# The gradients dK and dV of an attention block: dK on eight array tiles, two shared PSUM banks, and other places for three projections

## The chip, the core and the metric

The kernel runs on one core of a Trainium2 chip. A core has a tensor engine (PE, with its weight loads shown as PEld), a vector engine (DVE), a scalar engine (ACT), GpSimd (POOL), a queue engine that issues most transfers (SP), and 16 DMA engines. Each engine takes its instructions in order and waits on semaphores for the others. PE multiplies a stationary operand of up to 128 rows by 128 columns, loaded beforehand, by a moving operand that is streamed column by column, and writes into PSUM, eight banks of 128 partitions x 512 fp32 values. Its array can be used as tiles: a tile of 32x128 takes 32 rows of the contraction, a tile of 128x32 gives 32 output partitions, and sixteen tiles of 32x32 each have 32 rows and 32 output partitions of their own. Matmuls on different tiles can run at the same time.

The metric is the device time of one execution in microseconds (us).

## The reference

Two blocks read x (1 x 2048 x 448 each), and their outputs are concatenated. The kernel computes the outputs and all gradients for a given grad_out. Block A is linear attention with 16 heads; it is done in the first 205 us and is not touched. Block B is softmax attention with 16 query heads of 28 channels that share one key and one value head:

```
q = (x @ wq) as 16 heads;  k = x @ wk;  v = x @ wv          # one k, one v
p = softmax(q k^T * 28 ** -0.5);  o = p v;  out = o @ wo
# backward, with do = grad_out @ wo^T by head:
dV = sum over heads p^T do          dP = do v^T
dS = p * (dP - rowsum(do * o))      dQ = dS k        dK = sum over heads dS^T q
dx, dwq, dwk, dwv, dwo from dQ, dK, dV, o and x
```

All matmul operands are bf16, sums are fp32.

## The kernel before, in words

**Blocks and units.** The 2048 queries and 16 heads of block B are cut into 64 blocks, each of 256 queries and two heads. A block is worked off in eight units of 256 keys, so the main loop (L926) has 512 units of scores, numbered u, and 28 more in which the lagging steps run out. Loop and order of every engine are written out by hand (`tc.manual_schedule`, L917): the engines execute what the loop body issues, in that order. It runs from about 207 to 1017 us.

**One unit.** `rows_SD` (L683) issues eight matmuls on 32x128 tiles: the scores S of unit u for two heads, and dP of unit u-16. S of the first head goes to one of three banks SB (index 2u mod 3), of the second to the next of them; dP goes to the two banks DB. ACT takes the exponential of the first head's scores (L946), copies the second head's dP to SBUF as cp (L960), and takes the exponential of the second head (L992): three operations of 128x512 a unit. DVE multiplies the first head's dP by the stored exponentials (L958) and POOL the second head's cp (L961); both halves make dsT, the transposed dS. DVE transposes dsT in 32x32 blocks into dsx (L1039) for dK. Every fourth unit SP issues a DMA transpose of the exponentials, eT to eN (L994), for dV. In even units the second head's dP comes last in `rows_SD`.

**What follows in odd and even units.** In odd units come the four dK steps of `dk_m` (L860), for dsx of an older block (unit u-27), each four matmuls on four 32x32 tiles, 512 keys wide, all into the bank dk_acc. After the 32x32 transposes row group a of dsx holds, as rows, 32 queries, and as columns the keys 32a to 32a+31 of each 128; so the tile of row group a yields 32 channels of dK for 512 of the 2048 keys, in the output partitions from 32a. In even units come `o_dq` (L889: O and dQ on 128x32 tiles) and, at three of every four, one or two dV steps of `dv_mm` (L896), four matmuls on 128x32 tiles, 512 keys wide, into a bank dv_acc. Also in even units stand the PE transposes of O (`onat_T`, L809, u mod 8 = 2) and of do (`don_T`, L840, u mod 8 = 6) and the parts of the out-projection (L733). These use the score bank that is free at that time, `spare` = SB[(2u+2) mod 3] (L932), which is also the bank of the next unit's first scores.

**The do-projection.** do = grad_out @ wo^T is computed in 16 row tiles (`do_proj`, L903, and its copy to SBUF on DVE, `do_copy`, L913). Tiles 0 to 12 are done whole, four 128x512 matmuls, in the odd units 1 to 25; tiles 13 to 15 by quarters of 128 columns, 16 matmuls on 128x32 tiles each, in the units 32, 40, ... 120. The table is `do_slots` (L915). Before unit 16 the banks DB serve, then dk_acc until unit 27, then `spare` (L942).

**Transposes for dK's other operand.** For later blocks POOL copies queries into a staging tile qst (L851) at units 30, 31, 38, 39, 46, 47, 54, 55 of each 64; SP transposes it into qX behind the eN transposes in its queue.

**The end.** From unit 519 on, no scores are left, and dK uses a second bank, dk_two (SB[2]): the steps of odd m go to other output partitions of that bank, so that eight tiles work at a time. Matmuls for wo's gradient (`gwo`, L783, evicted at L793 and stored at L796) fill PE, and loads and transposes for the last stage are issued by SP. dv_acc is copied out at unit 533 (L1024, ACT), dk_two at unit 536 (L1030, ACT). After the loop dk_acc and the copy of dk_two are added in four DVE operations (L1059) into dkvT. Then rows of it are put into dQ's tile by 14 transfers (L1100, half on SP, half on POOL), and PE does `dwq` (L1063), the transposes of dK and dV, `dx` and the gradients of wk and wv.

Which tile of the array a dK matmul takes, and where it writes, is in this call:

```
mmt((dk_two if other else dk_acc)[k:k + 32, :],
    qX[qc][32 * a:32 * a + 32, B, s, pair * 64 + 32 * h:pair * 64 + 32 * h + 32],
    rhs, (32 * a, k), ...)        # (first row, first column) of the 32x32 tile
```

Of the kernel before, what the change touches and what calls it, by code (L numbers as in the profile page):

```python
# [8 lines left out]
ACT = mybir.ActivationFunctionType  # L9
ALU = mybir.AluOpType  # L10
AX = mybir.AxisListType
BF16 = mybir.dt.bfloat16
F32 = mybir.dt.float32
# [4 lines left out]
P = 128  # L18
# [7 lines left out]
def kernel(  # L26
# [21 lines left out]
    nc = tc.nc  # L48
# [3 lines left out]
    scale = float(DH) ** -0.5  # L52
# [586 lines left out]
    psA = psc.enter_context(tc.tile_pool(name="psA", bufs=4, space=bass.MemoryType.PSUM))  # L639
# [7 lines left out]
    NB = 64  # L647
# [3 lines left out]
    with ExitStack() as cs_:  # L651
        pe_ = cs_.enter_context(tc.tile_pool(name="ceT", bufs=1, side="right"))
        pn_ = cs_.enter_context(tc.tile_pool(name="ceN", bufs=1, side="right"))
        pd_ = cs_.enter_context(tc.tile_pool(name="cdsT", bufs=5, side="right"))
# [6 lines left out]
        SB = [psA.tile([P, 512], F32, name="aacc") for i in range(3)]  # L661
        DB = [psA.tile([P, 512], F32, name="agen") for i in range(2)]
        oq, dk_acc = (psA.tile([P, 512], F32, name="agen") for _ in range(2))

        dsT, dsx, qX, don, doT, rl, prod = ({} for _ in range(7))
# [6 lines left out]
        def eN(b, c):  # L672
            return ENs[(2 * b + c // 2) % 6][:, 16 * (c % 2):16 * (c % 2) + 16, :]

        def mmt(out, lhsT, rhs, pos, start, stop):
            nc.tensor.matmul(out, lhsT=lhsT, rhs=rhs, start=start, stop=stop, tile_position=pos,  # L676
                             skip_group_check=True)

        def blk(b):
            qc, pair = divmod(b, 8)  # L680
            return qc, pair, pair // 2, pair % 2
# [72 lines left out]
        post = {"gb": [], "xb": []}  # L754
# [100 lines left out]
            nc.sync.dma_start_transpose(qX[qc].rearrange("p b s c -> p (b s) c")[:, :, g * P:(g + 1) * P],  # L855
                                        st.rearrange("p n a j -> p (n a j)"))

        dk_two = SB[2]

        def dk_m(b, m, other=0):  # L860
            qc, pair, g, hp = blk(b)
            h, B, s = m // 8, (m // 2) % 4, m % 2
            for a in range(4):
                rhs = dsx[b][32 * a:32 * a + 32, :, h, :, :].rearrange(
                    "p u t (b i s) -> p u t b i s", b=4, s=2)[:, :, :, B, :, s]
                k = 32 * ((a + 2) % 4) if other else 32 * a
                mmt((dk_two if other else dk_acc)[k:k + 32, :],
                    qX[qc][32 * a:32 * a + 32, B, s, pair * 64 + 32 * h:pair * 64 + 32 * h + 32],
                    rhs, (32 * a, k), other == 2 or b == 0 and m == 0, other == 0 and b == NB - 1 and m == 15)

        def o_mm(v):
            b, tp = divmod(v, 8)
# [16 lines left out]
        def o_dq(vs, ys):  # L889
            for v, y in zip(vs, ys):  # L890
                todo = [f(i) for f, i in ((o_mm, v), (dq_mm, y)) if 0 <= i < NU]
                for _ in range(2):
                    for g_ in todo:
                        next(g_)

        def dv_mm(dv_acc, b, h, qb):  # L896
            for c in range(4):
                rhs = eN(b, c).rearrange("p (u h t q) k -> p u h t q k", u=2, h=2,
                                                       t=2)[:, :, h, :, qb, :]
                mmt(dv_acc[32 * c:32 * c + 32, :], don[b][:, qb, h, :], rhs, (0, 32 * c),  # L900
                    b == 0 and h + qb == 0, b == NB - 1 and h + qb == 2)

        def do_proj(i, c0, c1, ps):  # L903
            for c in range(4):
# [7 lines left out]
        def do_copy(i, c0, c1, ps):  # L912
            nc.vector.tensor_copy(out=do_nat[:, i, c0:c1], in_=ps[:, 0:c1 - c0])  # L913

        do_slots = {2 * i + 1: (i, 0, 512) for i in range(13)}  # L915
        do_slots.update({32 + 8 * n: (13 + n // 4, n % 4 * P, n % 4 * P + P) for n in range(12)})
        with tc.manual_schedule():  # L917
            nc.sync.dma_start(wo, wo_d[:, 0:D].rearrange("(g p) c -> p g c", p=P))
            qX[0] = pqa_.tile([P, 4, 2, 512], BF16, name="qX")
# [6 lines left out]
            for u in range(NU + 28):  # L926
# [5 lines left out]
                spare = SB[(2 * u + 2) % 3] if hasS else DB[u // 4 % 2] if u > 530 else SB[2]  # L932
# [6 lines left out]
                    out_proj(*op, spare)  # L939
                dpj = do_slots.pop(u, None)  # L940
                if dpj is not None:
                    dps_ = DB[u // 2 % 2] if u < 16 else dk_acc if u < 27 else spare  # L942
                    do_proj(*dpj, dps_)

                if hasS:
# [1 line left out]
                if u == 1:  # L947
                    q_shift(pn3, shifts[3], [pd_.tile([P, 2, 512], BF16, name="dsT").rearrange("p a b -> p (a b)").bitcast(F32)
                                             for _ in range(1)])
                    dv_acc = psA.tile([P, 512], F32, name="aacc")  # L950
                if u == 11:
                    for n in (2, 3):
                        put_shift(nc.sync, shifts[n], slice(n * 512, n * 512 + 512))
# [21 lines left out]
                if (b := due(u, 27)) is not None:  # L975
                    qc, pair, g, hp = blk(b)
                    nc.vector.tensor_scalar(out=qT_B[g][64 * hp:64 * hp + 64, qc * 256:(qc + 1) * 256],
                                            in0=oq[64:128, 0:256], scalar1=scale, scalar2=None, op0=ALU.mult)
# [20 lines left out]
                if u % 2:  # L999
                    b, i = divmod(u - 27, 8)  # L1000
                    if 0 <= b < NB:
                        for m in range(2 * i, 2 * i + 4):
                            dk_m(b, m, (1 + (u == 519 and m == 2 * i + 1)) * (m % 2) if 519 <= u < 537 else 0)
                else:
                    o_dq((u - 2, u - 1), (u - 20, u - 19))
                    b, n = divmod(u - 20, 8)
                    for k in {0: (0, 1), 2: (2,), 6: (3,)}.get(n, ()) if 0 <= b < NB else ():
                        dv_mm(dv_acc, b, k // 2, k % 2)
                y = u - 18

                if 512 <= u < 528 and u % 2 == 0:
# [6 lines left out]
                for v, half, gs in ((523, 0, (0, 1)), (525, 0, (2, 3)), (527, 1, (0, 1)), (529, 1, (2,)), (531, 1, (3,))):  # L1018
                    for g_ in gs if u == v else ():
                        nc.sync.dma_start_transpose(dqn[half][:, :, g_ * P:(g_ + 1) * P],  # L1020
                                                    qT_B[g_][:, half * 1024:half * 1024 + 1024])
                if u == 533:
                    for c in range(4):
                        nc.scalar.activation(out=post["dkvT"][32:64, c * 512:(c + 1) * 512], in_=dv_acc[32 * c:32 * c + 32, :],  # L1024
                                             func=ACT.Copy)
                if u == 536:
                    dk_sum = pd_.tile([P, 2, 512], BF16, name="dsT").rearrange("p a b -> p (a b)").bitcast(F32)
                    for c in range(2):
                        r = 64 * (1 - c)
                        nc.scalar.activation(out=dk_sum[64 * c:64 * c + 64, :], in_=dk_two[r:r + 64, :], func=ACT.Copy,  # L1030
                                             scale=scale)
                if u >= 519:
                    gwo(GW[u - 519], GW[u - 518])

                if 0 <= y < NU:
                    b, tp = divmod(y, 8)
                    if tp == 0:
                        dsx[b] = px_.tile([P, 8, 2, 2, 256], BF16, name="dsx")
                    nc.vector.transpose(  # L1039
                        out=dsx[b][:, tp, :, :, :].rearrange("p h t c -> p (h t c)").bitcast(F32),  # L1040
                        in_=dsT[y][:, :, :].rearrange("p h c -> p (h c)").bitcast(F32))

        dkvT, wqT, xb = post["dkvT"], post["wqT"], post["xb"]
# [10 lines left out]
            return pd_.tile([P, 2, 512], BF16, name="dsT")[:, 0, :]  # L1054

        for c in range(4):
            t = dkvT[0:32, :].rearrange("p (t a i) -> p t a i", a=4, i=32)[:, :, c, :]
            src = dk_acc[32 * c:32 * c + 32, :].rearrange("p (t i) -> p t i", i=32)
            nc.vector.scalar_tensor_tensor(out=t, in0=src, scalar=scale,  # L1059
                                           in1=dk_sum[32 * c:32 * c + 32, :].rearrange("p (t i) -> p t i", i=32),  # L1060
                                           op0=ALU.mult, op1=ALU.add)

        def dwq(c):  # L1063
            r = DC_ROWS[c]
# [44 lines left out]
        for c in range(4):  # L1109
            r = DC_ROWS[c]  # L1110
            ps = gen(0)
            for st in range(NS):
# [3 lines left out]
                                 func=ACT.Copy)  # L1116
# [35 lines left out]
```

## Time and profile before

| | |
|---|---|
| median of 3 runs | 1054.08 us (1053.51 to 1054.29) |
| profiled execution | 1052.68 us |
| its span | 1050.9 us |
| granted TensorE clock | 1.00 |
| PE busy | 1008.4 us, 96% |
| DVE busy | 895.9 us, 85% |
| ACT busy | 871.5 us, 83% |
| POOL busy | 798.2 us, 76% |
| dK matmuls of 32x512 into dk_acc | 4024 in the trace, 376 ns each, 264.0 us busy |
| dV matmuls of 128x512 | 1024, 379 ns each, 96.7 us busy |

A row of a group gives its line, engine, operation, the tiles written and read, the shape, the number of instructions, then busy time, mean duration of one, and the idle time of the engine ahead of them with what ended it. Matmuls overlap one another, on tiles above all, so a matmul's duration is not the time that it adds: the distance between starts is. The same holds for ACT and DVE operations, whose durations reach into the next operation. A timeline row gives the start within the span, the duration, and the group, where neighbours of one kind are put together with their number.

### The profile page before, as it was taken

The page shows a single profiled execution, that of the slowest core. Times are in us where ns is not written, and L with a number is a line of the kernel's source. Part 1 is how long each engine was busy: PE and PEld are TensorE (multiplying, and loading weights), DVE is VectorE, ACT ScalarE, POOL GpSimd, SP SyncE. Part 2 cuts the span into 40 slices and gives each one's busy share as a digit, 9 for nine tenths or more (in the row PEclk, how much of TensorE's full clock was granted, in tenths as well). Part 3 has the DMA queues.
Part 4 walks back from the last instruction along what each step waited for, and adds up shares of the span by engine and source line. Part 5 has one row for each costly group of instructions (what it writes and reads, how often), then busy time and mean ns, then how long its engine had stood idle before and what let it go on. Part 6 is the DMA issues. An engine that isn't in the chain of part 4 may idle for free.

```text
span 1050.9 us, 40033 instructions
## 1 busy us (share of the span) xinstructions
PE 1008.4 (96%) x16236; PEld 486.6 (46%) x16245; DVE 895.9 (85%) x1781; ACT 871.5 (83%) x1743; POOL 798.2 (76%) x1044
## 2 busy tenths in 40 slices
PE   9999999998999999999999999999999999999998
PEld 5555554434444444444444444444444444444444
DVE  6897500669999999999999999999999999999942
ACT  6463122589999999999999999999999999999632
POOL 8601272238888998899899989988998999888860
PEclk9999999999999999999999999999999999999999
DMA  9879999299999999999999999999999999999973
GB/s 266 150 134 192 189 222 215 42 163 202 188 196 190 188 195 198 194 193 191 197 175 195 192 202 185 204 199 184 192 194 191 194 190 193 204 186 182 220 156 87
DMA packets 689058, 195.15 MB, mean 186 GB/s; under 512 B 670408, under 2 KB 686688, under 8 KB 688872
## 3 DMA queue, kind: packets, MB, share of 16 engines
q1 hardware_dynamic: 680392, 179.97, 102.1%
q0 software_dynamic: 4544, 9.46, 3.4%
q10 hardware_dynamic: 3936, 3.16, 1.0%
q8 instruction: 127, 2.08, 0.8%
q14 instruction: 59, 0.48, 0.1%
HBM read 12.60 MB, written 10.84 MB: 22 GB/s over the span
## 4 chain that ended last, share of the span: by engine, by line
PE 44%; ACT 33%; issue 14%; DVE 6%; POOL 2%; DMA 0%; ACTq 0%; DVEq 0%; POOLq 0%
ACT cp L960 17%; ACT eT L992 13%; PE agen L81 13%; PE aacc L676 10%; PE agen L676 10%; PE aacc L81 6%; ACT eT L946 2%; DVE dsT L958 2%; PE aacc L809 2%; DVE dsx L1039 2%; PE aacc L840 1%; POOL dsT L961 1%; DMA out_dram<-dsT 0%; PE agen L313 0%; PE agen L227 0%
## 5 line engine op out<-in xcount | busy, mean ns | idle before, releaser
L961 POOL TENSOR_TENSOR dsT<-cp,eT 128x512 bf16<-128x512 bf16 x512 | 587.7, 1156 | 78.9 <-ACT cp L960 73.2
L1039 DVE STREAM_TRANSPOSE dsx<-dsT 128x512 f32<-128x512 f32 x512 | 357.8, 699 | 2.8 <-POOL dsT L961 0.7
L676 PEld LDWEIGHTS <-R 32*128 32x128 bf16 (+1 forms) x9104 | 228.5, 94 | 275.0 <-issue 239.4
L958 DVE TENSOR_TENSOR dsT<-agen,eT 128x512 bf16<-128x512 f32 x512 | 341.9, 668 | 10.6 <-PE agen L676 5.4
L960 ACT ACTIVATE cp<-agen 128x512 bf16<-128x512 f32 x512 | 315.8, 617 | 11.5 <-PE agen L676 10.5
L946 ACT ACTIVATE eT<-aacc 128x512 bf16<-128x512 f32 x512 | 313.6, 612 | 13.6 <-PE aacc L676 4.3
L992 ACT ACTIVATE eT<-aacc 128x512 bf16<-128x512 f32 x512 | 322.2, 629 | 0.0
L676 PE MATMUL agen<-dsx,qX 32*32 32x512 bf16 x4024 | 264.0, 376 | 0.0
L676 PE MATMUL agen<-doT,R 32*128 32x256 bf16 x2048 | 246.7, 269 | 4.2 <-DVE dsT L958 2.5
L676 PE MATMUL aacc<-R,R 32*128 32x256 bf16 (+1 forms) x2240 | 218.5, 269 | 7.1 <-DVE oTs L819 2.0
L676 PE MATMUL agen<-eT,R 128*32 128x256 bf16 x2048 | 157.4, 274 | 0.1
L676 PE MATMUL agen<-dsT,R 128*32 128x256 bf16 x2048 | 156.6, 274 | 0.1
L676 PEld LDWEIGHTS <-qX 32*32 32x32 bf16 x4096 | 78.2, 89 | 111.7 <-issue 53.3
L676 PE MATMUL aacc<-eN,don 128*32 128x512 bf16 x1024 | 96.7, 379 | 0.0
L81 PEld LDWEIGHTS <-R 128*128 128x128 bf16 x517 | 40.9, 98 | 42.2 <-issue 12.0
L81 PE MATMUL agen<-R,R 128*128 128x448 bf16 (+1 forms) x174 | 41.1, 360 | 1.8 <-ACT R L229 0.8
L851 POOL COPY qst<-R 128x512 bf16<-128x512 bf16 x56 | 34.2, 611 | 2.9 <-DMA qX<-qst 2.8
L823 POOL TENSOR_TENSOR prod<-R,oTs 128x128 f32<-128x128 bf16 x64 | 27.6, 431 | 9.3 <-DVE oTs L819 9.3
L676 PEld LDWEIGHTS <-don 128*32 128x32 bf16 x1024 | 33.8, 97 | 0.5
L586 DVE TENSOR_TENSOR osb<-R 32x512 bf16<-32x512 bf16 x4 | 1.7, 413 | 34.7 <-ACT R L583 34.7
L262 POOL TENSOR_SCALAR wdq<-wdq 128x448 bf16<-128x448 bf16 x16 | 21.1, 1327 | 12.9 <-DVE phiT L243 12.9
L427 POOL COPY pk<-R 128x256 bf16<-128x256 bf16 x4 | 1.6, 399 | 37.7 <-DVE R L389 37.7
(234 smaller groups left out, 983.1 us busy)
## 6 DMA issues: line engine op xcount, KB each, us to landing
eN<-eT SPq DMA_TRANSPOSE x128
xa<-in_A_x_dram SPq DMA_DIRECT2D x8, 224.0 KB
ga<-in_grad_out_dram SPq DMA_DIRECT2D x4, 448.0 KB
out_dram<-osb ACTq DMA_DIRECT2D x16, 112.0 KB
xa<-in_grad_out_dram POOLq DMA_DIRECT2D x4, 448.0 KB, 9.4
out_dram<-wdq POOLq DMA_DIRECT2D x8, 224.0 KB, 5.8
eT<-in_grad_out_dram SPq DMA_DIRECT2D x4, 448.0 KB
eT<-in_B_x_dram SPq DMA_DIRECT2D x4, 448.0 KB
```

Of the source, the lines that this page charges most:

```text
L81: nc.tensor.matmul(out_ap, lhsT=lhsT, rhs=rhs, start=start, stop=stop, tile_position=(0, 0))
L262: nc.gpsimd.tensor_scalar(out=wq_n[:, st, 0:D], in0=wq_n[:, st, 0:D], scalar1=1.0, scalar2=None, op0=ALU.min)
L676: nc.tensor.matmul(out, lhsT=lhsT, rhs=rhs, start=start, stop=stop, tile_position=pos, skip_group_check=True)
L809: nc.tensor.transpose(onp[:, qb, :, :].rearrange("p h c -> p (h c)"), oTs[0:64, qb * P:(qb + 1) * P], identF[0:64, 0:64], tile_position=(0 ...
L823: nc.gpsimd.tensor_tensor(out=prod[b][:], in0=dnv, in1=os_, op=ALU.mult)
L851: eng.tensor_copy(out=st.rearrange("p (b s) a j -> p b s a j", s=2)[:, :, s, :, :], in_=src.unsqueeze(2).to_broadcast([P, 4, 4, 32]))
L946: nc.scalar.activation(out=eT(u)[:, 0, :], in_=sp[0][:, :], func=ACT.Exp, scale=scale)
L958: nc.vector.tensor_tensor(out=dst[:, 0, :], in0=dp[0][:, :], in1=ew[:, 0, :], op=ALU.mult)
L960: nc.scalar.activation(out=cp[:, :], in_=dp[1][:, :], func=ACT.Copy)
L961: nc.gpsimd.tensor_tensor(out=dst[:, 1, :], in0=cp[:, :], in1=ew[:, 1, :], op=ALU.mult)
L992: nc.scalar.activation(out=eT(u)[:, 1, :], in_=sp[1][:, :], func=ACT.Exp, scale=scale)
L1039: nc.vector.transpose(out=dsx[b][:, tp, :, :, :].rearrange("p h t c -> p (h t c)").bitcast(F32), in_=dsT[y][:, :, :].rearrange("p h c -> p ...
```

## The change

dK is computed on eight 32x32 tiles at a time in the whole loop. Each step of four matmuls of 512 keys becomes eight of 256 keys: keys of the first half go to the bank dk_acc, keys of the second half to the bank that was dv_acc, at output partitions turned by two tiles (`dk_quad`). Each of the two banks (`kv_acc`) holds half of the keys of dK in its columns 0 to 255, and half of the keys of dV in its columns 256 to 511; dV's steps become eight matmuls of 256 keys on the same four 128x32 tiles, one half after the other. dk_two and the copies at units 533 and 536 are gone. After the loop sixteen evictions of 32x256 take the place of the four additions: the first bank's on DVE, the second bank's on ACT.

The do-projection is done whole for tiles 0 to 9 (units 1 to 19), and by quarters for tiles 10 to 15, in the odd units 37, 39, 45, 47, ... 125, 127, all in `spare`. So the whole ones at units 21, 23 and 25 and the quarters at units 32, 40, ... 120 are gone.

Lines after these move by five at most: L992 becomes L997, L1039 becomes L1034.

```diff
--- before.py
+++ after.py
@@ -855,18 +855,23 @@
             nc.sync.dma_start_transpose(qX[qc].rearrange("p b s c -> p (b s) c")[:, :, g * P:(g + 1) * P],
                                         st.rearrange("p n a j -> p (n a j)"))
 
-        dk_two = SB[2]
-
-        def dk_m(b, m, other=0):
+        KH = 256
+        kv_acc = [dk_acc]
+
+        def dk_quad(a, x):
+            return 32 * ((a + 2 * x) % 4)
+
+        def dk_m(b, m):
             qc, pair, g, hp = blk(b)
             h, B, s = m // 8, (m // 2) % 4, m % 2
-            for a in range(4):
-                rhs = dsx[b][32 * a:32 * a + 32, :, h, :, :].rearrange(
-                    "p u t (b i s) -> p u t b i s", b=4, s=2)[:, :, :, B, :, s]
-                k = 32 * ((a + 2) % 4) if other else 32 * a
-                mmt((dk_two if other else dk_acc)[k:k + 32, :],
-                    qX[qc][32 * a:32 * a + 32, B, s, pair * 64 + 32 * h:pair * 64 + 32 * h + 32],
-                    rhs, (32 * a, k), other == 2 or b == 0 and m == 0, other == 0 and b == NB - 1 and m == 15)
+            for x in range(2):
+                for a in range(4):
+                    rhs = dsx[b][32 * a:32 * a + 32, 4 * x:4 * x + 4, h, :, :].rearrange(
+                        "p u t (b i s) -> p u t b i s", b=4, s=2)[:, :, :, B, :, s]
+                    k = dk_quad(a, x)
+                    mmt(kv_acc[x][k:k + 32, 0:KH],
+                        qX[qc][32 * a:32 * a + 32, B, s, pair * 64 + 32 * h:pair * 64 + 32 * h + 32],
+                        rhs, (32 * a, k), False, b == NB - 1 and m == 15)
 
         def o_mm(v):
             b, tp = divmod(v, 8)
@@ -893,12 +898,12 @@
                     for g_ in todo:
                         next(g_)
 
-        def dv_mm(dv_acc, b, h, qb):
-            for c in range(4):
-                rhs = eN(b, c).rearrange("p (u h t q) k -> p u h t q k", u=2, h=2,
-                                                       t=2)[:, :, h, :, qb, :]
-                mmt(dv_acc[32 * c:32 * c + 32, :], don[b][:, qb, h, :], rhs, (0, 32 * c),
-                    b == 0 and h + qb == 0, b == NB - 1 and h + qb == 2)
+        def dv_mm(b, h, qb):
+            for x in range(2):
+                for c in range(4):
+                    rhs = eN(b, c).rearrange("p (u h t q) k -> p u h t q k", u=2, h=2, t=2)[:, x, h, :, qb, :]
+                    mmt(kv_acc[x][32 * c:32 * c + 32, KH:512], don[b][:, qb, h, :], rhs, (0, 32 * c),
+                        b == 0 and h + qb == 0, b == NB - 1 and h + qb == 2)
 
         def do_proj(i, c0, c1, ps):
             for c in range(4):
@@ -912,8 +917,8 @@
         def do_copy(i, c0, c1, ps):
             nc.vector.tensor_copy(out=do_nat[:, i, c0:c1], in_=ps[:, 0:c1 - c0])
 
-        do_slots = {2 * i + 1: (i, 0, 512) for i in range(13)}
-        do_slots.update({32 + 8 * n: (13 + n // 4, n % 4 * P, n % 4 * P + P) for n in range(12)})
+        do_slots = {2 * i + 1: (i, 0, 512) for i in range(10)}
+        do_slots.update({37 + 8 * (n // 2) + 2 * (n % 2): (10 + n // 4, n % 4 * P, n % 4 * P + P) for n in range(24)})
         with tc.manual_schedule():
             nc.sync.dma_start(wo, wo_d[:, 0:D].rearrange("(g p) c -> p g c", p=P))
             qX[0] = pqa_.tile([P, 4, 2, 512], BF16, name="qX")
@@ -939,7 +944,7 @@
                     out_proj(*op, spare)
                 dpj = do_slots.pop(u, None)
                 if dpj is not None:
-                    dps_ = DB[u // 2 % 2] if u < 16 else dk_acc if u < 27 else spare
+                    dps_ = DB[u // 2 % 2] if u < 16 else dk_acc if u < 20 else spare
                     do_proj(*dpj, dps_)
 
                 if hasS:
@@ -947,7 +952,7 @@
                 if u == 1:
                     q_shift(pn3, shifts[3], [pd_.tile([P, 2, 512], BF16, name="dsT").rearrange("p a b -> p (a b)").bitcast(F32)
                                              for _ in range(1)])
-                    dv_acc = psA.tile([P, 512], F32, name="aacc")
+                    kv_acc.append(psA.tile([P, 512], F32, name="aacc"))
                 if u == 11:
                     for n in (2, 3):
                         put_shift(nc.sync, shifts[n], slice(n * 512, n * 512 + 512))
@@ -1000,12 +1005,12 @@
                     b, i = divmod(u - 27, 8)
                     if 0 <= b < NB:
                         for m in range(2 * i, 2 * i + 4):
-                            dk_m(b, m, (1 + (u == 519 and m == 2 * i + 1)) * (m % 2) if 519 <= u < 537 else 0)
+                            dk_m(b, m)
                 else:
                     o_dq((u - 2, u - 1), (u - 20, u - 19))
                     b, n = divmod(u - 20, 8)
                     for k in {0: (0, 1), 2: (2,), 6: (3,)}.get(n, ()) if 0 <= b < NB else ():
-                        dv_mm(dv_acc, b, k // 2, k % 2)
+                        dv_mm(b, k // 2, k % 2)
                 y = u - 18
 
                 if 512 <= u < 528 and u % 2 == 0:
@@ -1019,16 +1024,6 @@
                     for g_ in gs if u == v else ():
                         nc.sync.dma_start_transpose(dqn[half][:, :, g_ * P:(g_ + 1) * P],
                                                     qT_B[g_][:, half * 1024:half * 1024 + 1024])
-                if u == 533:
-                    for c in range(4):
-                        nc.scalar.activation(out=post["dkvT"][32:64, c * 512:(c + 1) * 512], in_=dv_acc[32 * c:32 * c + 32, :],
-                                             func=ACT.Copy)
-                if u == 536:
-                    dk_sum = pd_.tile([P, 2, 512], BF16, name="dsT").rearrange("p a b -> p (a b)").bitcast(F32)
-                    for c in range(2):
-                        r = 64 * (1 - c)
-                        nc.scalar.activation(out=dk_sum[64 * c:64 * c + 64, :], in_=dk_two[r:r + 64, :], func=ACT.Copy,
-                                             scale=scale)
                 if u >= 519:
                     gwo(GW[u - 519], GW[u - 518])
 
@@ -1054,11 +1049,18 @@
             return pd_.tile([P, 2, 512], BF16, name="dsT")[:, 0, :]
 
         for c in range(4):
-            t = dkvT[0:32, :].rearrange("p (t a i) -> p t a i", a=4, i=32)[:, :, c, :]
-            src = dk_acc[32 * c:32 * c + 32, :].rearrange("p (t i) -> p t i", i=32)
-            nc.vector.scalar_tensor_tensor(out=t, in0=src, scalar=scale,
-                                           in1=dk_sum[32 * c:32 * c + 32, :].rearrange("p (t i) -> p t i", i=32),
-                                           op0=ALU.mult, op1=ALU.add)
+            for x in range(2):
+                k = dk_quad(c, x)
+                t = dkvT[0:32, :].rearrange("p (x t a i) -> p x t a i", x=2, a=4, i=32)[:, x, :, c, :]
+                src = kv_acc[x][k:k + 32, 0:KH].rearrange("p (t i) -> p t i", i=32)
+                tv = dkvT[32:64, c * 512 + KH * x:c * 512 + KH * x + KH]
+                sv = kv_acc[x][32 * c:32 * c + 32, KH:512]
+                if x:
+                    nc.scalar.activation(out=t, in_=src, func=ACT.Copy, scale=scale)
+                    nc.scalar.activation(out=tv, in_=sv, func=ACT.Copy)
+                else:
+                    nc.vector.tensor_scalar(out=t, in0=src, scalar1=scale, scalar2=None, op0=ALU.mult)
+                    nc.vector.tensor_copy(out=tv, in_=sv)
 
         def dwq(c):
             r = DC_ROWS[c]
```

## The prediction

> **What bounds the kernel now.** I read the page first, then a table of busy time by stretch, then the timeline of single units of the main loop, then the chain of waits where a unit was longer than its neighbours. The page:
>
> ```profile
> PE 1008.4 (96%) x16236; PEld 486.6 (46%) x16245; DVE 895.9 (85%) x1781; ACT 871.5 (83%) x1743; POOL 798.2 (76%) x1044
> ...
> PE 44%; ACT 33%; issue 14%; DVE 6%; POOL 2%; DMA 0%; ACTq 0%; DVEq 0%; POOLq 0%
> ...
> L676 PE MATMUL agen<-dsx,qX 32*32 32x512 bf16 x4024 | 264.0, 376 | 0.0
> ```
>
> It names TensorE at 96%, and dK as its costliest matmul group. By that reading halving dK would pay enormously. The table of the main loop says otherwise:
>
> ```profile
> core 0: us, PE busy (x) PEld busy (x) DVE busy (x) ACT busy (x) POOL busy (x), PEclk, DMA share, GB/s
> 400.00:984.00 584.00, 564.25 (x11048) 265.62 (x11047) 571.03 (x1111) 575.38 (x1155) 527.76 (x636) 1.00 1.17 192
> ```
>
> ACT is busy 575.38 of 584 us (98.5%), DVE 97.8%, PE 96.6%: three engines within 2% of one another, with ACT ahead. One odd unit and the even one after it show who waits for whom:
>
> ```profile
> 602.76 0.82 PE L676 MATMUL agen<-dsx,qX 32*32 32x512 bf16 x12
> ...
> 603.04 0.60 ACT L960 ACTIVATE cp<-agen 128x512 bf16<-128x512 f32 x1
> ...
> 603.51 0.28 PE L676 MATMUL aacc<-R,R 32*128 32x256 bf16 x2
> 603.52 0.62 ACT L992 ACTIVATE eT<-aacc 128x512 bf16<-128x512 f32 x1
> ...
> 603.64 0.43 PE L676 MATMUL agen<-doT,R 32*128 32x256 bf16 x3
> ...
> 603.99 0.63 ACT L946 ACTIVATE eT<-aacc 128x512 bf16<-128x512 f32 x1
> ```
>
> ACT's three operations of a unit start 476 ns apart (603.04, 603.52, 603.99), each before the one ahead has ended: 1.43 us a unit at least, 11.44 for eight. dK ends and the even unit's scores start at 603.51. The last two of that unit's dP matmuls write the bank that cp is read from; cp ends at 603.645 and they start at 603.697 and 603.805 (in the group at 603.64). So after dK PE waits for ACT anyway. The starts of the second exponential over the whole loop repeat every eight units: 1.50, 1.43, 1.70, 1.43, 1.61 (1.50 in the other head pair), 1.43, 1.50, 1.43, that is 12.03 or 11.97 us. Every step from an odd unit to an even one, the one with dK in it, stands at ACT's 1.43. All excess lies in the steps from even to odd, behind dQ, dV and the transposes. The 1.70, for example, is the transpose of O, which starts 51 to 55 ns after the second exponential of the unit before it ends, then dQ, dV and the next scores in a row.
>
> **Part 1, dK in eight tiles.** Now: 16 matmuls of 512 columns in four rounds of four tiles, 230 ns and then 217 ns between rounds, 0.98 us from the first to the next scores (310.62 to 311.60 below). Then: 32 matmuls of 256 columns in four rounds of eight. The tail of this trace already uses eight tiles:
>
> ```profile
> 988.74 0.41 PE L676 MATMUL agen<-dsx,qX 32*32 32x512 bf16 x4
> 988.75 0.41 PE L676 MATMUL aacc<-dsx,qX 32*32 32x512 bf16 x4
> ```
>
> Both banks start together, and the next eight start 231 ns later, so eight of 512 take what four took. Eight of 256 would take about 109 ns if the columns set it. Issue must then keep 16 instructions (loads included) in 109 ns, 6.8 ns each; the do-projection's quarter at 315.20 goes at 55 ns for eight, 6.9 ns each. I take 0.55 us for the block, 0.43 less. In 246 of 256 blocks (the others are the tail's) this ends in a longer wait for cp: gain 0. Bounds: −0.05 us a block, all that lies between cp's end and the matmul that waits for it, −12 us in all, and 0; more gain is excluded, since cp's end does not move by it, and more cost needs a block longer than today's (rival C). I take 0: the two matmuls already go at the 109 ns of their columns.
>
> The Trainium skill ("TensorE: Matmul & The Clock Gate", Part 3, The mechanism) says that a weight load overlaps running matmuls only where its row group differs. The new round uses each row group twice, so by it a round would take two passes, 217 ns, and dK would stay at 0.98 us. The rows at 988.74 speak against it. By either figure the sum's term is 0, as the 0.98 us fits today.
>
> **Part 2, dV by halves.** A dV of four 512-column matmuls (217 ns) becomes two rounds of 109 ns: 218, and one more start. I take 1.3 ns for each of 256, +0.3 us; bounds 0 and 4 ns, 0 to +1.0 us. It is on the path behind the O transpose.
>
> **Part 3, the do-projections.** Gone are the full ones at units 21, 23 and 25: DVE copies of 691 ns (L913), and steps of 1.83, 2.18 and 1.83 us near them where 1.50 to 1.70 is usual, some 1.3 us. But just behind them POOL stands still:
>
> ```profile
> 264.92 1.90 issue
> ...
> 266.84 0.13 POOL qst L851
> ```
>
> At 266.84 (unit 38) the qst copy waits for a transpose landing. It is queued on SP behind the eN transposes (L994), 5.0 to 5.6 us each, back to back from 214 to about 333 us. They do not come sooner because units 21 to 25 do, so the time gained is lost there: 0 (bounds −1.5 and 0). The new quarters at 37, 39, 45 and 47 are absorbed by that wait and the like one at 278.3.
>
> The 12 quarters that stood in units 32, 40 to 120 cost nothing now: the step is 1.50 or 1.51 with one or without. So nothing comes back for them but their 208 ns of DVE.
>
> Open are ten pairs, in units 53, 55 to 125, 127. A quarter's bank is the spare score bank; the next unit's first scores write the same one, so they must wait for the copy on DVE. Unit 69 shows what that means:
>
> ```profile
> 309.99 0.65 ACT L992 ACTIVATE eT<-aacc 128x512 bf16<-128x512 f32 x1
> ...
> 310.98 0.65 DVE L958 TENSOR_TENSOR dsT<-agen,eT 128x512 bf16<-128x512 f32 x1
> ...
> 311.56 0.69 DVE L1039 STREAM_TRANSPOSE dsx<-dsT 128x512 f32<-128x512 f32 x1
> 311.60 0.28 PE L676 MATMUL aacc<-R,R 32*128 32x256 bf16 x2
> ...
> 312.08 0.62 ACT L946 ACTIVATE eT<-aacc 128x512 bf16<-128x512 f32 x1
> ```
>
> The bank is free at 310.63 (309.99 + 0.65); the quarter takes 0.41 us (315.20's row), to 311.09, and dK's saving pays for that. But DVE has begun dsT at 310.98 and can copy only at 311.56, for 0.29: scores at 311.90 where they started at 311.60, exponential at 312.33 (0.42 after the scores, as at 608.21 and 608.62) where it started at 312.08. That is 0.25 us for a pair's first quarter; by the other head pair's rows (unit 77: DVE free at 323.47, first exponential 324.00) 0.24. Queued behind that copy on DVE is the dsx transpose (L1039), 0.21 us later; its readers come nine units on. For the second quarter: in unit 71 DVE is free early and the copy ends before its scores are due, 0; in unit 79 dsT runs from 325.84 to 326.41, the copy ends at 326.70, scores 326.75, exponential 327.17 where it started at 326.97: 0.20. All later gates hang on ACT, so a delay stays. Sum: 10 × 0.245 + 5 × 0.20 = 3.4. Part may be taken back in the even units that DVE sets (unit 122 has 1.93 for 1.70, two units behind a quarter that goes away: −0.23). I take +2.9; bounds +1.0 and +5.
>
> **Part 4, the tail.** From unit 519 eight tiles are in use already; only the last block, 1016.20 to 1017.18, gets shorter: −0.42. Gone from ACT are four copies of dV (587 ns each) and two of dK; from DVE four L1059, 2.78 us in one row from 1017.29. New, after the loop: eight evictions of 32x256 on DVE, about 0.41 each by the nearest row (64x256 copies, 405 and 427 ns), 3.3 us; and eight on ACT, estimated at 0.39 from 512-column copies of 587 and 56-column ones of 217, 3.1 us. The scheduler puts the last grad-wo eviction (L793, now at 1018.84) behind seven of these: about 1019.5, and the first dwq on that bank waits 0.7 to 0.9. All seven POOL issues of the padding rows (L1100, 0.5 to 0.6 each) now stand behind the four of L796, so the last one lands about 3 us later than at 1025.2, when PE comes to dx. Three dwq matmuls move ahead of unit 531's dK; their transposes were issued by 1000.0 and PE is there at 1006.5. Net +0.2; bounds −0.6 and +2.
>
> **Sum.** 0 + 0.3 + 0 + 2.9 + 0.2 = +3.4 us. The profiled execution took 1052.68 us (span 1050.9 and 1.8 around it): 1056.1. The median shown is 1054.08, 1.4 above it, so on the scale of the medians 1057.5.
>
> **The rivals.**
> A, faster: PE's relief does reach the path, where the last two dP matmuls wait for cp, because an emptier array lets them and dQ behind them go sooner. It outweighs the +3.4 from 14 ns a block on; at 30 ns, −7.4 and −4.0 in all, 1050.1. For it speaks the chain's 44% on PE; against it the 109 ns between the two matmuls now. The whole excess of eight units over 11.44 is 0.53 to 0.59 us, 36 us in 64 times eight; none of it begins at dK.
> B, no change: DVE's slack and the lost even quarters take back the quarters' delay: +1.0 + 0.3 − 0.4 = +0.9, about 1055. For it: unit 122. Against: units 70 and 78 start ACT's chain late, and ACT's starts are then 476 ns apart again, with nothing to catch up in.
> C, much slower: eight-tile rounds of 256 columns are bound by loads and issue. At a round of 217 ns nothing changes. The cover is from 603.51 to cp's end, some 0.13 us; beyond about 250 ns a round each further 10 ns costs 256 × 0.04 = 10 us. At 270 ns: +20, 1077. For it: twice the loads per column, and mean weight loads of 89 ns. Against: 6.9 ns an instruction at 315.20.
> D, slower at the end: the tail takes its upper bound, +2, with the quarters at +5: +7.5, 1061.5.
>
> **How the numbers follow.** Forecast (+1.5 to +5.5) 0.48, A 0.20, B 0.15, C 0.04, D 0.13. No change that can be measured is within 0.2% of 1054.08, ±2.1 us: B whole, 0.07 of the forecast's low side and 0.02 of A, 0.24. Faster is the rest of A, 0.18; slower 0.58. The forecast's own range is 1055.6 to 1059.6; the range given leaves out C and half of A: 1050.5 to 1062.
>
> **What would show it.** dK blocks of 0.5 to 0.6 us and PE's busy share falling by some 100 us, while the odd-to-even steps stay at 1.43; the scores of units 54, 62 to 126 starting behind a DVE copy, with the step before them 0.2 to 0.25 longer; POOL's wait at 266.84 longer by what units 21 to 25 gave; L793's last eviction near 1019.5. The prediction is wrong if even-to-odd steps away from the quarters change, or if the round of eight is not near 109 ns.

## The result and the profile after

The changed kernel takes 1159.78 us (median of 4 runs, 1153.67 to 1167.96), the kernel before 1053.8 us beside it. The ratio is 1.101, with a 95% interval of 1.094 to 1.108: 106 us slower, where the forecast had 3.4 and a range up to 1062. The profiled execution took 1159.96 us.

The page of the changed kernel, its busy times, its instruction transfers and its dK groups:

```profile
PE 1029.9 (89%) x21545; PEld 560.2 (48%) x21545; DVE 905.6 (78%) x1794; ACT 880.8 (76%) x1745; POOL 801.2 (69%) x1044
...
PEclk9999999988898889988998899989889998998999
...
q8 instruction: 168, 2.75, 0.9%
...
L676 PE MATMUL aacc<-dsx,qX 32*32 32x256 bf16 x4096 | 186.2, 291 | 27.3 <-issue 27.2
L676 PE MATMUL agen<-dsx,qX 32*32 32x256 bf16 x4096 | 184.7, 290 | 12.4 <-issue 12.3
```

No engine is busy all the time: the busiest has 89%, where PE had 96% before. The TensorE clock, full all through before, has slices of 0.8. And the dK matmuls have idle time ahead of them that is put down to "issue", that is, to no wait that the profile shows. Before, the dK matmuls had none. The line of queue 8 is easily passed over. It counts the transfers that bring instructions: 168 packets and 2.75 MB, where the kernel before has this line:

```profile
q8 instruction: 127, 2.08, 0.8%
```

The same window of the main loop as before, first the table of busy time, then the waits:

```profile
core 0: us, PE busy (x) PEld busy (x) DVE busy (x) ACT busy (x) POOL busy (x), PEclk, DMA share, GB/s
400.00:984.00 584.00, 508.44 (x13199) 281.34 (x13197) 507.28 (x980) 514.83 (x1023) 469.34 (x564) 0.93 1.02 171
```

```profile
PEld L676 <- issue: 245.3, 790, 4.3
POOL dsT L966 <- ACT cp L965: 107.3, 190, 4.2
ACT eT L951 <- PE agen L676: 64.6, 55, 4.5
DVE dsT L963 <- PE agen L676: 54.8, 61, 4.5
PE aacc L676 <- issue: 32.3, 23, 4.0
```

The columns of a wait are the waiting engine and line, what it waited for, us in all, how often, and the longest. Before, ACT waited for PE 0.5 us in this window, and PE's weight loads never over 0.4 us for "issue". Now single stretches reach 4 us, and PE is what the others wait for. One of them on the timeline:

```profile
269.28 0.35 PEld L676 LDWEIGHTS <-qX 32*32 32x32 bf16 x29 [0.20 <-issue]
...
269.64 0.28 PE L676 MATMUL agen<-dsx,qX 32*32 32x256 bf16 x4
269.66 0.28 PE L676 MATMUL aacc<-dsx,qX 32*32 32x256 bf16 x1
...
272.25 0.09 PEld L676 LDWEIGHTS <-qX 32*32 32x32 bf16 x3 [2.62 <-issue]
272.26 0.29 PE L676 MATMUL aacc<-dsx,qX 32*32 32x256 bf16 x3 [2.32 <-issue]
```

PE stops in the middle of a round of eight dK matmuls. Five are done, three are missing, and they come 2.6 us later. The eight have the same inputs and write the same two banks, so a semaphore would have held the round and not its last three matmuls; an empty instruction queue can stop anywhere. A packet of queue 8 holds 16,384 bytes. A row of the PE program is a load or a matmul; the trace has 43,090 of them (32,481 before), which over 168 packets are 256 each. (The expectations below count some 180 rows fewer in each kernel: 42,900 and 32,300 here.) Numbered in the order of the trace, the rows at which PE resumes after its first long gaps in the main loop are 4012, 4268, 4524, 5035, 5802, 6057 and 6313: 256 or a multiple of it apart, within one. By a gap I mean more than 0.6 us from the start of one PE row to the start of the next. I also compared each gap's end with the packets' times. Of the 62 gaps between 240 us and the tail, where no scores are left, 59 end 1.2 to 1.65 us after a packet has arrived, and these make 89.3 us in all. In the kernel before there are 5 gaps, 3.9 us, and none ends like that.

What the stop does to the clock is in a table of narrow windows around it:

```profile
258.00:269.60 11.60, 9.16 (x292) 5.28 (x289) 9.94 (x20) 9.82 (x20) 9.56 (x13) 1.00 1.20 196
269.60:272.70 3.10, 0.78 (x32) 0.26 (x16) 1.38 (x3) 1.29 (x3) 1.91 (x2) 1.00 1.20 150
272.70:276.10 3.40, 3.40 (x74) 1.68 (x66) 2.42 (x6) 2.38 (x5) 1.96 (x4) 0.50 1.24 238
276.10:282.00 5.90, 5.40 (x180) 3.48 (x179) 5.77 (x12) 5.83 (x13) 4.82 (x6) 1.00 1.22 177
```

At full clock PE stands still; then it has its instructions again, but at clock 0.50 for 3.4 us. The changed kernel has 27 such windows of 3.4 or 6.8 us, 140 us in all. (Two of them, at 242 us and at the very end, 10 us together, have their like in the run with half transposes below, which has no others.) I took the steps from one second exponential to the next, from unit 32 to 510, less the step that the same unit of the kernel before usually has. Sorted by what falls into the step, this excess is: with a gap alone 31 us, with half clock alone 20, with both 55, with neither 6. Together 111.5; the same reckoning gives 5.0 for the kernel before. The difference, 106.5 us, is the whole result.

Two theories remain. **Supply**: PE uses up its instructions faster than they come, and the clock falls because PE stands still. **Density**: eight tiles at once, or what they leave idle, bring the clock down, and the gaps follow.

### The profile page after: what moved, and what is told of

Its sections match the earlier page's. It is cut to its first block, busy times and chain, and to the rows that moved or that the text cites. A ratio compares the mean times of both kernels' runs of the same rounds, so it can differ in the third digit from the quotient of the medians.

```text
span 1158.2 us, 50675 instructions
## 1 busy us (share of the span) xinstructions
PE 1029.9 (89%) x21545; PEld 560.2 (48%) x21545; DVE 905.6 (78%) x1794; ACT 880.8 (76%) x1745; POOL 801.2 (69%) x1044
## 3 DMA queue, kind: packets, MB, share of 16 engines
q8 instruction: 168, 2.75, 0.9%
## 5 line engine op out<-in xcount | busy, mean ns | idle before, releaser
L963 DVE TENSOR_TENSOR dsT<-agen,eT 128x512 bf16<-128x512 f32 x512 | 344.8, 673 | 94.2 <-PE agen L676 89.3
L676 PEld LDWEIGHTS <-R 32*128 32x128 bf16 (+1 forms) x9296 | 252.4, 96 | 301.5 <-issue 263.6
L1034 DVE STREAM_TRANSPOSE dsx<-dsT 128x512 f32<-128x512 f32 x512 | 358.2, 700 | 2.1 <-POOL dsT L966 0.2
L997 ACT ACTIVATE eT<-aacc 128x512 bf16<-128x512 f32 x512 | 318.2, 621 | 0.0
L676 PE MATMUL agen<-doT,R 32*128 32x256 bf16 x2048 | 276.6, 286 | 12.8 <-DVE dsT L963 2.5
L676 PE MATMUL aacc<-R,R 32*128 32x256 bf16 (+1 forms) x2432 | 266.1, 280 | 19.4 <-issue 3.3
L676 PE MATMUL aacc<-dsx,qX 32*32 32x256 bf16 x4096 | 186.2, 291 | 27.3 <-issue 27.2
L676 PE MATMUL agen<-dsx,qX 32*32 32x256 bf16 x4096 | 184.7, 290 | 12.4 <-issue 12.3
L676 PEld LDWEIGHTS <-qX 32*32 32x32 bf16 x8192 | 97.5, 92 | 112.0 <-issue 105.7
L676 PE MATMUL aacc<-eN,don 128*32 128x256 bf16 x1024 | 82.0, 290 | 4.6 <-issue 4.6
L676 PE MATMUL agen<-eN,don 128*32 128x256 bf16 x1024 | 81.9, 290 | 4.4 <-issue 4.4
L676 PEld LDWEIGHTS <-don 128*32 128x32 bf16 x2048 | 65.5, 103 | 14.7 <-issue 11.1
L676 PE MATMUL aacc<-wo,R 128*32 128x112 bf16 (+1 forms) x720 | 20.7, 229 | 13.7 <-issue 9.1
```

Of the source, the lines that this page charges most:

```text
L963: nc.vector.tensor_tensor(out=dst[:, 0, :], in0=dp[0][:, :], in1=ew[:, 0, :], op=ALU.mult)
L997: nc.scalar.activation(out=eT(u)[:, 1, :], in_=sp[1][:, :], func=ACT.Exp, scale=scale)
L1034: nc.vector.transpose(out=dsx[b][:, tp, :, :, :].rearrange("p h t c -> p (h t c)").bitcast(F32), in_=dsT[y][:, :, :].rearrange("p h c -> p ...
```

## The experiments

**Eight tiles without more instructions.** To the kernel before:

```diff
-dk_m(b, m, (1 + ...) * (m % 2) if 519 <= u < 537 else 0)
+dk_m(b, m, (1 + ...) * (m % 2) if 519 <= u < 537 else 3 * (m % 2))
-mmt((dk_two if other else dk_acc)[k:k + 32, :], ...
+mmt((dv_acc if other == 3 else dk_two if other else dk_acc)[k:k + 32, :], ...
```

> The kernel before, with dK on eight 32x32 tiles at a time in the whole loop, but with 512 columns a matmul, so that PE has as many instructions as before (32,300 rows, against 42,900 of the changed kernel). To have a second bank, the steps of odd m write into dv_acc; so dK and dV are not computed rightly here, the work is the same. Supply theory (PE runs dry because its instructions, which arrive in packets of 16,384 bytes or 256 rows, are used up faster than they come: gaps of 0.8 us and more stand 256 instructions apart in the changed kernel's trace, and the trace of before has none in its main loop): no gaps, clock 1.00, 1054 us, within 2. It also tests the forecast's own step, that a shorter dK block gains nothing: then 1052 to 1056; if PE's relief reaches the path, below 1050. Density theory (eight tiles at once make the clock drop, which the changed kernel shows as windows of 0.5, and the gaps follow from that): windows of 0.5 as in the changed kernel, mean clock 0.94, 1120 us or more.

Measured: 1052.94 us, ratio 0.9991 (0.9981 to 1.0000). No gap ends behind a packet, and the clock is 1.00. So eight tiles at once do not bring the clock down by themselves; that short matmuls on eight tiles might is left to the run with half transposes below. The run also confirms the forecast's first step: dK's blocks are half as long and the time moves by at most 0.2%.

**More instructions without eight tiles.** To the kernel before, up to unit 518:

```diff
+for x in range(2):                    # keys 256 x .. 256 x + 255, same bank, same tile
     for a in range(4):
-        rhs = dsx[b][32 * a:32 * a + 32, :, h, :, :]...
+        rhs = dsx[b][32 * a:32 * a + 32, 4 * x:4 * x + 4, h, :, :]...
-        mmt(dk_acc[k:k + 32, :], ...)
+        mmt(dk_acc[k:k + 32, 256 * x:256 * x + 256], ...)
```

> The kernel before, with dK on four tiles as it was, but each matmul of 512 columns cut into two of 256 in the same bank up to unit 518: 40,173 rows on PE, no eight tiles, no shared banks, do-projections as before. PE streams as many columns in as many passes as before. Supply theory: gaps at every 256th row, clock windows of 0.5, some 75% of the changed kernel's loss or more (7,870 of its 10,600 added rows): 1115 to 1165 us. Density theory: no eight tiles, so no loss: 1053 to 1056.

Measured: 1124.49 us (1116.23 to 1130.71), ratio 1.0665 (1.0625 to 1.0704). The timeline of one stop:

```profile
373.99 0.50 PE L676 MATMUL agen<-dsx,qX 32*32 32x256 bf16 x9
...
375.74 0.54 PEld L676 LDWEIGHTS <-qX 32*32 32x32 bf16 x21 [1.54 <-issue]
375.74 0.72 PE L676 MATMUL agen<-dsx,qX 32*32 32x256 bf16 x17 [1.26 <-issue]
```

Nine matmuls of a block are done, then PE stops in the middle of a group again. 46 of its 51 gaps (59.3 us) end 1.2 to 1.65 us after a packet. So twice the instructions for dK's columns, without eight tiles or shared banks, cost 71 us. The clock, though, is 0.99 here and 0.94 in the changed kernel: its half-clock windows follow gaps of 2.0 us and more, those of the changed kernel gaps from 1.2 on. That dK's shorter blocks leave PE idler around a gap fits this, but was not tested by itself.

**Half of those instructions.** The same cut in every second block only.

> The kernel before with dK's matmuls cut into two of 256 columns on four tiles, in every second block only: 36,204 rows on PE, half of the rows added in the run that cut all (40,173 rows, 1124 us). Supply theory: in the blocks with cuts 256 rows last 5.2 us, in the others 6.7, and a shortage can be made up in the others: some third to half of that run's +71 us, 1070 to 1095. Density theory: 1053 to 1056.

Measured: 1072.99 us, ratio 1.0194 (1.0176 to 1.0213), +20 us. 11 gaps behind a packet, 13.2 us. The loss is not in proportion: 3,900 more rows cost 20 us, 7,870 cost 71.

**dV by halves alone.** The kernel before, with dV's eight matmuls of 256 columns in its own bank.

> The kernel before with dV alone cut by halves of the keys (eight matmuls of 256 columns in its own bank): 34,348 rows on PE, 492 in eight units of the loop for 460. 256 rows then last 6.2 us instead of 6.7. The forecast had +0.3 us (0 to 1.0) for this. Supply theory: between the 6.7 us of the kernel before (no gap of 0.8 us in the loop's middle) and the 5.2 us of the run with dK cut in two (gaps, +71 us) there is a threshold; at 6.2 us few gaps: 1053 to 1065. Density theory: 1053 to 1055.

Measured: 1054.77 us, ratio 1.0014 (1.0005 to 1.0023): +1.5 us (0.5 to 2.4). Of its ten gaps three end 1.2 to 1.65 us after a packet, 2.1 us. This leaves the forecast's 0.3 for the rounds possible, and it suggests that supply begins to be short here, at 34,500 rows.

**What makes the packets late.** The changed kernel, with less for the DMA engines to do from unit 24 on:

```diff
-dma_start_transpose(ENs[u // 4 % 6][:, :, :], ETs[...]...)
+nb = 32 if u < 24 else 16
+dma_start_transpose(ENs[u // 4 % 6][:, 0:nb, :], ETs[...]...[:, 0:nb * P])
```

> The changed kernel, with the DMA transposes of the exponentials cut to half from unit 24 on (16 of 32 column blocks; the other half of eN keeps old values, so dV is not computed rightly). PE, ACT, DVE and POOL do the same work. If the packets of instructions come late because they stand behind these transposes (4.9 to 5.4 us each, the DMA engines 0.9 to 1.07 busy), their wait gets shorter, the gaps go, the clock stays at 1.00 and the forecast's sum holds: 1054 to 1062 us. If supply is short whatever else the DMA engines do (or density is the cause), it stays at 1150 to 1165.

Measured: 1053.29 us, ratio 1.0001 (0.9990 to 1.0011), a little under the range that was expected, with all 43,000 rows on PE. No gap is left from 240 us to the tail, and from 400 to 900 us the clock is 1.00. Its waits from 400 to 900 us:

```profile
PEld L676 <- issue: 175.8, 774, 0.4
POOL dsT L966 <- ACT cp L965: 41.7, 133, 0.5
```

The longest "issue" is 0.4 us, as before the change. So it is not the number of instructions as such, nor short matmuls on eight tiles: the packets come in time once the transposes leave room. With both, more instructions and full transposes, they don't. Density falls.

**The same bytes in smaller pieces, first try.** The changed kernel, whole:

```diff
-if u % 4 == 3:
-    dma_start_transpose(ENs[u // 4 % 6][:, :, :], ETs[u // 4 % 5]...)
+if u % 2:
+    uh = u % 4 // 2
+    dma_start_transpose(ENs[u // 4 % 6][:, 16 * uh:16 * uh + 16, :], ETs[u // 4 % 5][:, 2 * uh:2 * uh + 2]...)
```

> The changed kernel, whole and right, with each DMA transpose of four units' exponentials issued as two of two units each, at every second unit: as many bytes, half as long each. If a packet of instructions waits for the one transpose that is ahead of it in the DMA engines' queues, its wait halves (2.7 us in the mean now from the use of the packet before, 1.3 with half the bytes), and most gaps go: 1056 to 1080 us. If it waits because the DMA engines are loaded as they are, whatever the pieces: 1140 to 1165, or slower by what the smaller transposes cost.

Measured: 1422.27 us, which no theory had. From 560 to 680 us, waits of SP and then of PE:

```profile
SPq L1000 <- PE aacc L676: 19.4, 7, 3.6
```

```profile
PE agen L676 <- DMA eN<-eT: 33.6, 7, 6.0
```

The first piece, now issued two units sooner, stands on SP until PE has read its slot for the last time; the pieces behind it come late, and then dV waits for them, some 5 us in every block. No gap ends behind a packet any more (0 of 62), but this run made a wait of its own and can't price the packets'.

**Second try.** First piece when it was issued before, second piece two units later.

> The changed kernel, whole and right, with each transpose of four units' exponentials in two pieces again, but the second piece is issued two units later than now, not the first piece two units sooner. In the run before this one the first piece had to wait on SP for PE's last reader of its slot (19.4 us in 120), PE then waited for the transposes (about 5 us in every block), and no gap stood 256 rows apart; so that run told of its own wait, and not how long a packet of instructions waits. Here the slot is free in time, and a transpose has 11 units until dV reads it. If a packet waits for the one transpose ahead of it, gaps shrink: 1060 to 1110 us. If the DMA engines' load sets it, no better than the changed kernel: 1140 to 1180. If PE waits for the transposes again (the groups of dV behind DMA): above 1200.

Measured: 1107.82 us (1104.47 to 1112.34), ratio 1.0511 (1.0485 to 1.0536), nearly half of the loss gone. Of 40 gaps over 0.6 us 2 end behind a packet (1.4 us), where the changed kernel has 59. What is left is of another kind; its waits from 400 to 900 us:

```profile
PEld L676 <- issue: 190.6, 718, 3.0
POOL dsT L966 <- ACT cp L965: 40.6, 113, 1.8
POOL qst L851 <- DMA qX<-qst: 34.7, 12, 5.4
```

POOL's copy waits for the qX transpose in SP's now longer queue, and the others behind that. As many bytes, in pieces half as long, let the packets through. The load of the DMA engines as such is not the cause: from 400 to 900 us they move 179 GB/s here and 169 in the changed kernel. As a mend it is no use, for it pays with SP's queue.

**The wait itself, in the same traces.** The gaps tell which row is the first of a packet: one in 256, on a grid that slips by some 50 rows over the loop (the trace has some 90 more rows of PE that are neither loads nor matmuls). So one can take, for each packet of the main loop from 300 us on, the time from PE's first row of the packet before it to the packet's own start. (The grid is good to some ten rows, 0.2 us; kernels without gaps are given the grid of those with them.) A packet takes 0.95 us, and 1.2 us is the least from its end to its first row on PE. What 256 rows last undisturbed, less these two, is by estimate the latest start without a gap:

| run | 256 rows last | latest start | mean start | longest | later than the latest |
|---|---|---|---|---|---|
| before | 6.7 us | 4.5 us | 1.7 us | 3.9 us | 0 of 98 |
| dV by halves | 6.2 us | 4.0 us | 1.9 us | 4.3 us | 4 of 104 |
| dK cut, four tiles | 5.2 us | 3.0 us | 2.5 us | 4.6 us | 50 of 126 |
| changed kernel | 5.0 us | 2.8 us | 2.7 us | 4.8 us | 70 of 135 |
| transposes in two pieces, second try | 5.0 us | 2.8 us | 1.5 us | 3.8 us | 2 of 134 |
| half transposes | 5.0 us | 2.8 us | 0.9 us | 2.7 us | 0 of 133 |

Before the change, too, a packet started up to 3.9 us after that row, but there this was still in time. Shorter transposes make the start sooner, as they would if a packet waits for the burst that is ahead of it. More rows leave less time to wait.

**The do-projections, two ways.** Only the new `do_slots` in the kernel before, and the same in the kernel with eight tiles of 512 columns.

> The kernel before with the new places of the do-projection alone (whole ones up to unit 19, 24 quarters in the odd units 37 to 127), +360 rows on PE. The forecast had +2.9 us (1.0 to 5) for them, with dK's block shortened by 0.43; here dK still takes 0.98 us, so the quarter's 0.41 us of PE comes on top in odd units: in unit 69 the quarter ends at 311.09, dK at 312.07, the next scores start 0.47 us late; 20 units by 0.3 to 0.5, +6 to +10, 1060 to 1064. Supply theory: more rows in units 53 to 127 only, few or no gaps. Density theory: the same.

> The eight-tile dK of 512 columns (dK and dV not computed rightly, as there; 1052.9 us, 32,300 rows on PE) with the new places of the do-projection: the quarters' price with dK's block short, as the forecast had it, and with instructions in supply (32,660 rows). Forecast's step: +2.9 us (1.0 to 5) against that run, 1054 to 1058; the changed kernel with half transposes shows the steps behind a quarter 0.24 and 0.10 to 0.23 longer and the ones after 0.04 shorter, 0.25 and 0.38 us for a pair, +3.1. If the quarters are free once dK is short: 1052 to 1053.5.

Measured: 1061.78 us with the long dK (ratio 1.0073, 1.0059 to 1.0088, +7.7 us), 1056.85 us with the short one (ratio 1.0035, 1.0022 to 1.0048; 3.9 us above the run without the quarters, or 4.6 by the two ratios). The second lies within the forecast's term, 2.9 with bounds of 1.0 and 5.

## Why the prediction was wrong

**The step that failed** is the price of the instructions themselves, which Part 1 put at 0 (bounds −12 us and 0) and which came to some 106 us. "16 instructions (loads included) in 109 ns, 6.8 ns each" asked if PE can issue that fast for one block, and it can: in the changed kernel four rounds start at 604.91, 605.03, 605.15 and 605.26 and the block is over at 605.50, 0.59 us, as forecast. I never asked whether 43,090 rows instead of 32,481 reach PE in time. They come in packets of 256 rows through the DMA engines, which were busy 0.9 and more of the time in the loop before the change. Before, 256 rows lasted 6.7 us of the loop (460 rows in 12 us); after, 5 us (620 rows). Rival C, "bound by loads and issue", was the only one that pointed this way, but it looked for the limit inside a round and ended at 1077. The queue-8 line of before, 0.8% of the DMA engines' time, looks like little, but it is a share of throughput, and here the wait of a single packet decides.

**The other terms held, as far as the runs can tell.** The run with half transposes shows them on the changed kernel's own instructions. Its time as a whole does not show the forecast's sum: +0.0 us (−1.1 to +1.2) for +3.4. But half the transposes is also less work than the sum was made for, so the sum itself stays untested. Its unit 69:

```profile
310.23 0.41 PE L676 MATMUL aacc<-R,R 128*32 128x128 bf16 x16
...
310.53 0.65 DVE L963 TENSOR_TENSOR dsT<-agen,eT 128x512 bf16<-128x512 f32 x1
...
311.10 0.27 DVE L918 CAST R<-aacc 128x128 bf16<-128x128 f32 x1
...
311.43 0.28 PE L676 MATMUL aacc<-R,R 32*128 32x256 bf16 x2 [0.20 <-DVE R L918]
...
311.84 0.60 ACT L951 ACTIVATE eT<-aacc 128x512 bf16<-128x512 f32 x1
```

The quarter is done at 310.64, DVE is in dsT until 311.10, and the scores wait for the copy behind it. The step is 1.67 us for 1.43, +0.24 where the forecast had 0.25; the second quarter's is +0.10 or +0.23, for 0 or 0.20, and the step after it 0.04 shorter. Ten pairs make +3.1, against 2.9 forecast; from unit 52 to 128 the loop takes 2.8 us longer than before.

- dK off the path: confirmed. In undisturbed stretches of the changed kernel (units 160 to 167) the steps are 1.46, 1.43, 1.70, 1.43, 1.61, 1.43, 1.50, 1.43, the pattern of before but for the first, and eight tiles alone gave 0.9991. But PE's busy time did not fall by the forecast 100 us: 994.9 us with eight tiles alone and 996.9 with half transposes, against 1008.4. A dK matmul of half the columns still has 274 ns in the profile of the run with half transposes, for 376, so most of the busy time of short matmuls is not columns.
- The tail: ACT's evictions took 0.375 us each (forecast 0.39), DVE's 0.417 (0.41), and PE's wait for L793 was 0.78 (0.7 to 0.9):

```profile
1127.58 0.54 ACT L793 ACTIVATE dsT<-aacc 128x448 bf16<-128x448 f32 x1
...
1128.17 3.40 PE L81 MATMUL aacc<-eN,eT 128*128 128x448 bf16 x16 [0.78 <-ACT dsT L793]
```

  From the last exponential's start to the end of the span it is 73.4 us for 72.9: +0.5, forecast +0.2. How near that is may be luck: with half transposes, which has the tail of the changed kernel, it is 72.3, and with eight tiles alone, which has the tail of before, 72.2. So a term of this size is not resolved.
- The early wait at 266.84, said to grow by what units 21 to 25 gave, was not seen so: with gaps from 258.8 us on, the copy came late itself, at 268.64.
- In rival D the upper bounds add up to +7.3 (0.3, 5 and 2), not to +7.5.
- The rule on weight loads ("TensorE: Matmul & The Clock Gate", Part 3, The mechanism), weighed in the forecast, does not hold here. The round uses each row group twice, and still takes 0.11 to 0.12 us, as forecast from the 109 ns of its columns.

The Trainium skill has a rule that bears on the second half of the loss. The same page, "HAM oscillation — how this bites in real kernels", puts it as no idle gaps of PE longer than about 3.4 us. By the measurement this limit is too high here: the windows at 0.50, 3.4 or 6.8 us long, mostly follow single gaps of 1.2 to 2.6 us among otherwise busy PE, and they go when the gaps go. Not every such gap has one: behind a gap of 2.1 us at 698 us the clock stays at 1.00.

## What to carry to other kernels

Before cutting matmuls into more and smaller ones, count the instructions per microsecond of the loop, not only the columns. Here 256 PE rows in 5 us instead of 6.7, beside DMA engines that are nearly full of transposes, cost 10%, and what the cut was to win was never on the path. Idle time put down to "issue" that falls into the middle of a group, every 256 instructions, and ends soon after a packet of the instruction queue, points to an empty queue. Here either fewer instructions or shorter transfers ahead of the packets helped, and a wait that ends in a half-clock window is dearer than it looks.

## What the runs showed of the hardware that was not expected

- PE's instructions come in packets of 16,384 bytes, 256 rows. PE resumed 1.2 to 1.65 us after a packet's end in 59 of 62 gaps of the changed kernel.
- The loss grows steeply with the rows: 32,481 rows 0 us, 34,529 +1.5, 36,385 +20, 40,353 +71, with dK or dV only cut finer.
- A packet takes about 0.95 us itself; it is its start that is late. With the transposes halved, 43,000 rows came through with no gap over 0.6 us; with transposes in two pieces (second try), 2 gaps ended behind a packet instead of 59.
- After many of the gaps the clock stands at 0.50 for 3.4 or 6.8 us: 140 us in the changed kernel (mean 0.94), 24 us with dK cut on four tiles (0.99).
- Eight 32x32 tiles writing two banks take 8 x 256 columns in 0.11 to 0.12 us, each row group loaded twice.
